# One tile's layernorm statistics moved to ScalarE, a shorter TensorE warm-up and a new matmul order in an FFT-plus-GLU kernel

## Chip, cores and metric

The kernel runs on one core of one Trainium2 chip. The metric is the device time of one execution in microseconds, lower is better. Every run quoted here was fast, with a granted TensorE clock of 0.999 or 1.0 of full speed. A number called "median" is over the executions of one kernel in one comparison; the span of a profile is some 1.8 us shorter than the time of the run that it was taken in.

## The reference, cut to what matters

```python
def reference(A_x, A_w_r, A_w_i, B_x, B_w_gate, B_w_up, B_w_down):
    # A_x: 1 x 2048 x 640 bf16; w_r, w_i: 2048 x 321; w_gate, w_up: 640 x 1536; w_down: 1536 x 640
    xn = _layernorm(A_x, axis=-1)                    # (x - mean) / sqrt(var + 1e-5), per row
    X  = rfft2(xn) * (A_w_r + 1j * A_w_i)            # ... cut: in float32
    a  = irfft2(X)                                   # ... cut
    h  = (xn @ w_gate) * (xn @ w_up)                 # the GLU, F = 1536
    return A_x + a + h @ w_down
```

Everything waits for the layernorm, and TensorE does all the rest: the gated linear unit (GLU), and the Fourier transforms as matmuls with constant tables.

## The kernel before

The source does not list instructions in order. It declares tasks with an engine, an estimated duration, a priority and dependencies, and a list scheduler orders the tasks of each engine and counts PSUM banks for each class of task. The core then runs each engine's list in that order, with semaphore waits (in e8, below, VectorE stood 1.53 us in front of a copy whose input was there). A change to a priority or an estimate therefore changes orders, and nothing else.

Rows 16p+b form tile b, so there are 16 tiles of 128 rows. Tiles 0 to 3 are loaded by one transfer each and transposed by TensorE; tiles 4 to 7 come in one transfer, 8 to 15 in another, and are transposed by DMA. The parts that the change touches:

```python
xv = A_x[0].rearrange("(p j) d -> p j d", j=16)
sch.caps = {"glu": opts.get("cap_glu", 2), "acc": opts.get("cap_acc", 4), "fill": 1}   # PSUM banks per class
# ... cut
for fi in range(opts.get("nfill", 70)):            # filler, planned into early gaps of TensorE
    def em_fill(c):                                # two matmuls of 128 columns on zeros
        # ... cut
nwarm = opts.get("nwarm", 12)
def em_warm(c):                                    # warm-up: 4 * nwarm matmuls of 128 columns on zeros
    # ... cut
T("warm", "pe", opts.get("warm_ns", 5050.0), em_warm, prio=-1.0, ...)
# ... cut: statistics of tile b
if b >= opts.get("act_stats", 6):                  # tiles 6 to 15: two passes on ScalarE
    # activation(Copy, scale=1/640, accum_out=mean), activation(Square, bias=mean, accum_out=sum of squares)
else:                                              # tiles 0 to 5: VectorE, two bn_stats of 320 columns, one bn_aggr
    if 1 <= b <= 3: bns[0].deps.add(muls[b - 1])   # not before the tile ahead is normalised
    if b == 1:      bns[1].deps.add(e0_first)      # second half after tile 0's transposes are copied out
# ... cut: add epsilon (VectorE), square root (ScalarE), reciprocal, subtract, multiply (VectorE)
# T0_b: five transposes of tile b; eT0_b: the copy of them out of PSUM, in two parts for b < 2,
#       columns 0..255 on ScalarE and 256..639 on VectorE
w_at = [6.0 + opts.get("w_rate", 2.2) * min(ft // 2, 4) for ft in range(12)]      # when weights are expected
gu = T("GU_%d_%d" % (ft, b0), "pe", ..., bank="single", cls="glu")                # ten GLU matmuls: 5 gate, 5 up
eg = T("eG_%d_%d" % (ui, u), ("act", "dve"), ..., frees=gu)                       # evacuates them, frees the bank
```

The names used below: a **GLU matmul** is one of GU's matmuls of 128 or 256 columns. The **first length-64 transform** is the first stage of the Fourier part after the early GLU work (L1034 before, L1048 after), some 89 us into the span. From there to the end TensorE does the same matmuls in the same order in both kernels, except for the last few accumulations.

## Time and profile before

| | before |
|---|---|
| time, median of 3 runs | 206.84 us (206.67 to 207.27) |
| span of the profile | 204.3 us |
| TensorE busy | 199.7 us, 98% |
| VectorE, ScalarE busy | 178.7 us, 121.4 us |
| tile 0's transposes start | 6.04 us |
| first GLU matmul | 7.54 us |
| tile 3's transposes start | 14.32 us, after 100 GLU matmuls |
| first length-64 transform | 88.9 us |

The page and the timeline behind this table are shown and read in the prediction. These are rows of the 40 equal slices of the span, 5.1 us each: the busy share of the DMA engines in tenths, and what they moved.

```profile
DMA  6999993603139460001333343225033122324212
GB/s 179 301 342 383 387 210 15 67 0 64 32 66 242 86 202 0 3 0 27 66 65 60 68 113 65 65 70 158 0 98 113 55 76 83 112 80 111 83 35 62
```

From the second to the sixth slice the DMA engines are busy for 90% or more, moving 300 to 390 GB/s for most of it.

### The profile page before, as it was taken

Reading aid. Unit: us, or ns where it says so; the run is one execution under the profiler, and the core shown is the slowest. Engines: PE = TensorE matmul, PEld = TensorE weight load, DVE = VectorE, ACT = ScalarE, POOL = GpSimd, SP = SyncE. Lnnn points to the kernel's source line nnn. Section 1 sums busy time; section 2 is a strip of 40 time slices with the busy share of each in tenths; the row PEclk is TensorE's granted clock in tenths of the full one; section 3 lists DMA queues with packets and bytes.
Section 4 is the critical chain, followed back from the end, with each engine's and each line's share of the span. In section 5 each row is a group of like instructions: output and inputs, shape, how many; then the busy total and the mean of one; then the engine's idle time right before and its main releaser. Section 6 shows DMA issues by size and latency. Waiting matters only on the chain.

```text
span 204.3 us, 4499 instructions
## 1 busy us (share of the span) xinstructions
PE 199.7 (98%) x1681; PEld 137.2 (67%) x1695; DVE 178.7 (87%) x508; ACT 121.4 (59%) x282; POOL 21.8 (11%) x36
## 2 busy tenths in 40 slices
PE   7999999999999999999999999999999999999995
PEld 7998999554545455465777666666777787777774
DVE  3798999999999999949997997818999999999973
ACT  2379998999976577577999899878420222000000
POOL 0000000000000000003655365310000000000000
PEclk9999999999999999999999999999999999999999
DMA  6999993603139460001333343225033122324212
GB/s 179 301 342 383 387 210 15 67 0 64 32 66 242 86 202 0 3 0 27 66 65 60 68 113 65 65 70 158 0 98 113 55 76 83 112 80 111 83 35 62
DMA packets 30740, 21.69 MB, mean 106 GB/s; under 512 B 10752, under 2 KB 29696, under 8 KB 30592
## 3 DMA queue, kind: packets, MB, share of 16 engines
q1 hardware_dynamic: 29920, 21.06, 40.6%
q10 hardware_dynamic: 800, 0.36, 0.6%
q8 instruction: 13, 0.21, 0.4%
q14 instruction: 7, 0.06, 0.1%
HBM read 16.82 MB, written 2.62 MB: 95 GB/s over the span
## 4 chain that ended last, share of the span: by engine, by line
PE 92%; DVE 6%; issue 1%; ACT 1%
PE ps L969 36%; PE ps L1229 26%; PE ps L989 13%; DVE arena L1070 3%; PE ps L747 3%; PE ps L930 2%; PE ps L1146 2%; PE ps L1239 2%; PE ps L1034 2%; PE ps L1117 2%; PE ps L1118 2%; DVE arena L1073 1%; PE ps L1058 1%; PE ps L1055 1%; PE ps L1057 1%; PE ps L1056 1%
## 5 line engine op out<-in xcount | busy, mean ns | idle before, releaser
L719 ACT ACTIVATE arena<-ps 128x512 bf16<-128x512 f32 (+5 forms) x183 | 97.1, 568 | 48.7 <-PE ps L1146 23.4
L969 PE MATMUL ps<-arena 128*128 128x512 bf16 x346 | 80.1, 379 | 0.9 <-DVE arena L1073 0.3
L969 PEld LDWEIGHTS ps<-arena 128*128 128x128 bf16 x360 | 33.9, 98 | 36.5 <-ACT arena L719 0.8
L1229 PE MATMUL ps<-arena 128*128 128x320 bf16 (+2 forms) x396 | 56.7, 295 | 0.0
L1229 PEld LDWEIGHTS ps<-arena 128*128 128x128 bf16 x396 | 38.0, 98 | 13.9
L989 PE MATMUL ps<-arena 128*128 128x128 bf16 (+1 forms) x360 | 28.2, 237 | 0.1
L989 PEld LDWEIGHTS ps<-arena 128*128 128x128 bf16 x360 | 24.9, 98 | 2.5 <-ACT arena L719 0.7
L1070 DVE TENSOR_TENSOR arena<-ps,arena 128x256 f32<-128x256 f32 x64 | 22.6, 414 | 1.4 <-PE ps L1058 1.2
L1005 DVE TENSOR_TENSOR arena<-arena 128x512 bf16<-128x512 bf16 x36 | 15.3, 425 | 9.0 <-ACT arena L719 8.8
L1093 POOL TENSOR_TENSOR arena<-arena 128x256 bf16<-128x256 f32 x16 | 10.3, 644 | 111.5 <-DVE arena L1086 111.5
L1249 DVE TENSOR_TENSOR arena<-ps,arena 128x320 bf16<-128x320 f32 (+2 forms) x33 | 15.3, 473 | 3.8 <-PE ps L1239 3.8
L1094 POOL TENSOR_TENSOR arena<-arena 128x256 bf16<-128x256 f32 x16 | 11.9, 745 | 0.0
L1117 PE MATMUL ps<-arena 128*128 128x128 bf16 x80 | 10.4, 219 | 0.1
L1118 PE MATMUL ps<-arena 128*128 128x128 bf16 x80 | 10.4, 219 | 0.0
L1117 PEld LDWEIGHTS ps<-arena 128*128 128x128 bf16 x80 | 8.7, 111 | 1.7
L1118 PEld LDWEIGHTS ps<-arena 128*128 128x128 bf16 x80 | 8.7, 112 | 1.4
L1239 PE MATMUL ps<-arena 128*128 128x320 bf16 (+2 forms) x33 | 9.1, 295 | 0.0
L883 DVE TENSOR_TENSOR arena<-arena 128x384 f32<-128x384 bf16 x16 | 8.8, 551 | 0.0
L773 ACT ACTIVATE arena<-arena 128x640 bf16<-128x640 bf16 x10 | 8.3, 825 | 0.0
L782 DVE BATCH_NORM_STATS2 arena<-arena 128x6 f32<-128x320 bf16 x12 | 5.4, 481 | 2.8 <-DMA arena<-in_A_x_dram 2.7
L767 ACT ACTIVATE arena<-arena 128x640 bf16<-128x640 bf16 x10 | 7.3, 734 | 0.3 <-DMA arena<-in_A_x_dram 0.2
L1073 DVE TENSOR_TENSOR arena<-ps,arena 128x260 f32<-128x260 f32 x16 | 7.0, 438 | 0.0
(72 smaller groups left out, 235.7 us busy)
## 6 DMA issues: line engine op xcount, KB each, us to landing
arena<-in_A_x_dram SPq DMA_DIRECT2D x20, 160.0 KB, 2.5
out_dram<-arena SPq DMA_DIRECT2D x31, 80.0 KB, 1.6
arena<-c_tf SPq DMA_DIRECT2D x4, 384.0 KB, 11.2
arena<-in_A_w_r_dram SPq DMA_DIRECT2D x32, 40.1 KB, 2.3
arena<-in_A_w_i_dram SPq DMA_DIRECT2D x32, 40.1 KB, 2.3
arena<-in_B_w_gate_dram SPq DMA_DIRECT2D x4, 320.0 KB, 5.4
arena<-in_A_x_dram SPq DMA_DIRECT2D x1, 1280.0 KB, 10.3
arena<-c_ti SPq DMA_DIRECT2D x2, 512.0 KB, 4.9
```

The source lines that it names most:

```text
L719: return c.e.activation(dst, src, _ACTF.Copy)
L969: ins = c.e.matmul(ps[:, bk, :], v_gw[:, w, j, ft, :], v_xt[:, j, rows], start=(j == 0), stop=(j == 4))
L989: ins = c.e.matmul(ps[:, bk, w * n:(w + 1) * n], v_gw[:, w, j, ft, :], v_xt[:, j, rows], start=(j == 0), stop=(j == 4))
L1005: return c.e.tensor_tensor(v_ht[:, ft0, rows], v_gbf[:, rr, 0, :], v_gbf[:, rr, 1, :], _OP.mult)
L1070: c.e.tensor_tensor(v_p[:, ar, w, :, 128 * h:128 * h + 128].rearrange("p c (m k) -> p c m k", k=4), xh.rearrange("p c (m k) -> p c m k", k ...
L1093: c.e.tensor_tensor(v_y[ar][:, 512:768], p01[:, 0:256], p10[:, 0:256], _OP.add)
L1094: return c.e.tensor_tensor(v_y[ar][:, 256:512], p00[:, 0:256], p11[:, 0:256], _OP.subtract)
L1117: c.e.matmul(dst, l1, v_ti[:, t, 0, :], start=True, stop=False)
L1118: ins = c.e.matmul(dst, l2, v_ti[:, t, 1, :], start=False, stop=True)
L1229: ins = c.e.matmul(ps[:, bk, 0:sl3.stop - sl3.start], v_ht[:, ft, a * 128:(a + 1) * 128], v_wd[:, ft, sl3], start=(ft == 7 and px is None) ...
L1239: return c.e.matmul(ps[:, bank_of(own), 0:sl3.stop - sl3.start], v_sm[:, 2, :], v_v[:, a, sl3], start=False, stop=True)
L1249: return c.e.tensor_tensor(v_out[:, a % 2, sl3], ps[:, bk, 0:sl3.stop - sl3.start], v_xr[:, xs, sl3], _OP.add)
```

## The change

Its intent: have TensorE start useful work sooner. Tile 1 is normalised earlier, because its statistics run on ScalarE while VectorE is busy with tile 0; the warm-up ends before tile 0 is ready instead of after it; the filler is cut finer and is tied behind tile 0's transposes; and a third PSUM bank with new priorities lets more 128-column GLU matmuls come early.

```diff
@@ -564,6 +564,7 @@
 
         sch = _Sched()
         sch.caps = {"glu": opts.get("cap_glu", 2), "acc": opts.get("cap_acc", 4), "fill": 1}
+        sch.caps["glu2"] = opts.get("cap_glu2", 3)
         sch.caps["a"] = opts.get("cap_a", 2)
         lay = {}
         cur = [0]
@@ -730,15 +731,18 @@
         def em_wz(c):
             return c.e.memset(v_dum, 0.0)
         T("warm_zero", "dve", 150.0, em_wz, writes=[(b_dum, None)], prio=-1.0)
+        fills = []
         for fi in range(opts.get("nfill", 70)):
             def em_fill(c):
                 bk = bank_of(c.t)
-                c.e.matmul(ps[:, bk, 0:128], v_dum[:, 0:128], v_dum[:, 128:256], start=True, stop=True)
-                return c.e.matmul(ps[:, bk, 128:256], v_dum[:, 0:128], v_dum[:, 128:256], start=True,
-                                  stop=True)
-            T("fill%d" % fi, "pe", 2 * _d_mm(128), em_fill, prio=90.0 + 0.001 * fi, bank="single", cls="fill",
-              selffree=True, reads=[(b_dum, None)])
-        nwarm = opts.get("nwarm", 12)
+                ins = None
+                for i in range(4):
+                    ins = c.e.matmul(ps[:, bk, 64 * i:64 * i + 64], v_dum[:, 0:128], v_dum[:, 128:192], start=True,
+                                     stop=True)
+                return ins
+            fills.append(T("fill%d" % fi, "pe", 2 * _d_mm(128), em_fill, prio=90.0 + 0.001 * fi, bank="single", cls="fill",
+              selffree=True, reads=[(b_dum, None)]))
+        nwarm = opts.get("nwarm", 10)
 
         def em_warm(c):
             bk = bank_of(c.t)
@@ -747,7 +751,7 @@
                 ins = c.e.matmul(ps[:, bk + (i % 2), (i % 4) * 128:(i % 4 + 1) * 128], v_dum[:, 0:128],
                                  v_dum[:, 128:256], start=True, stop=True)
             return ins
-        T("warm", "pe", opts.get("warm_ns", 5050.0), em_warm, reads=[(b_dum, None)], prio=-1.0,
+        T("warm", "pe", opts.get("warm_ns", 4280.0), em_warm, reads=[(b_dum, None)], prio=-1.0,
           bank="pair", cls="warm", selffree=True)
 
         def em_wpad(c):
@@ -759,15 +763,20 @@
             dma("ld_x%d" % gi, v_x[:, b0:b0 + nb, :], xv[:, b0:b0 + nb, :], 128 * nb * (1800 if nb == 4 else 1400 if nb == 1 else 1280),
                 [(b_x, ("s", b0, b0 + nb))], prio=(0.0, 0.003, 0.02, 0.03, 0.042, 0.06)[gi])
         muls = {}
+        sd0 = None
+        aset = set(opts.get("act_set", (1,))) | set(range(opts.get("act_stats", 6), 16))
         for gi, (b0, nb) in enumerate(_LN_GROUPS):
             pbase = 1.0 + 0.05 * gi if gi < 4 else opts.get("ln_prio", 5.99) + 0.05 * (gi - opts.get("ln_lead", 4))
             for b in range(b0, b0 + nb):
-                if b >= opts.get("act_stats", 6):
+                if b in aset:
                     def em_sm(c, b=b):
                         return c.e.activation(v_jk, v_x[:, b, :], _ACTF.Copy, scale=1.0 / _D,
                                               accum_out=v_m32[:, b:b + 1])
-                    T("sm%d" % b, "act", _d_act(640) + 93, em_sm, reads=[(b_x, ("s", b, b + 1))],
+                    sm_ = T("sm%d" % b, "act", _d_act(640) + 93, em_sm, reads=[(b_x, ("s", b, b + 1))],
                       writes=[(b_m32, ("b", b, b + 1)), (b_jk, None)], prio=pbase)
+
+                    if b < 4 and sd0 is not None:
+                        sm_.deps.add(sd0)
 
                     def em_sq(c, b=b):
                         return c.e.activation(v_jk, v_x[:, b, :], _ACTF.Square, scale=-1.0, bias=v_m32[:, b:b + 1],
@@ -784,14 +793,14 @@
                                      writes=[(b_st, ("b", 2 * b + i, 2 * b + i + 1))], prio=pbase))
                     if 1 <= b <= 3:
                         bns[0].deps.add(muls[b - 1])
-                    if b == 1:
+                    if b == 1 and opts.get("bn1_split", 1):
                         bns[1].deps.add(e0_first)
 
                     def em_ag(c, b=b):
                         return c.e.bn_aggr(v_mv[:, b, :], v_st[:, b, :])
                     T("ag%d" % b, "dve", 176.0, em_ag, reads=[(b_st, ("b", 2 * b, 2 * b + 2))],
                       writes=[(b_mv, ("b", b, b + 1))], prio=pbase)
-            if b0 >= opts.get("act_stats", 6):
+            if b0 in aset:
                 def em_mb(c, sl_=slice(b0, b0 + nb)):
                     c.e.tensor_copy(v_mv[:, sl_, 0], v_m32[:, sl_])
                     return c.e.tensor_scalar(v_mv[:, sl_, 1], v_ss[:, sl_], 1.0 / _D, None, _OP.mult)
@@ -806,7 +815,9 @@
 
             def em_sd(c, sl_=sl_):
                 return c.e.activation(v_sd[:, sl_], v_ve[:, sl_], _ACTF.Sqrt)
-            T("sd_%d" % gi, "act", 200.0, em_sd, reads=[(b_ve, gk)], writes=[(b_sd, gk)], prio=pbase - 0.006)
+            sd_ = T("sd_%d" % gi, "act", 200.0, em_sd, reads=[(b_ve, gk)], writes=[(b_sd, gk)], prio=pbase - 0.006)
+            if gi == 0:
+                sd0 = sd_
 
             def em_rs(c, sl_=sl_):
                 return c.e.reciprocal(v_rs[:, sl_], v_sd[:, sl_])
@@ -846,6 +857,9 @@
                     return ins
                 t0 = T("T0_%d" % b, "pe", 5 * _d_mm(128), em_t0, reads=[(b_x, ("s", b, b + 1)), (b_sm, ("t", 0, 1))],
                        prio=pb, bank="pair" if b < opts.get("e0_split", 2) else "single", cls="a")
+                if b == 0:
+                    for f in fills:
+                        f.deps.add(t0)
 
                 if b < opts.get("e0_split", 2):
                     for part, (j0, j1) in (("act", (0, 2)), ("dve", (2, 5))):
@@ -855,7 +869,7 @@
                             src = psb[:, o_: o_ + (j1 - j0) * 128].rearrange("p (j s) -> p j s", s=128)
                             return copy_on(c, v_xt[:, j0:j1, b * 128:(b + 1) * 128], src)
                         n_ = (j1 - j0) * 128
-                        es_ = T("eT0_%d_%s" % (b, part), part, {"dve": _d_dve_psum16(n_), "act": _d_act(n_)}, em_e0s,
+                        es_ = T("eT0_%d_%s" % (b, part), (part, "dve") if part == "act" else part, {"dve": _d_dve_psum16(n_), "act": _d_act(n_)}, em_e0s,
                                 writes=[(b_xta if j0 == 0 else b_xtb, ("s", b * 128, (b + 1) * 128))], prio=pb - 0.001, frees=t0)
                     hold(t0, es_)
                     if b == 0:
@@ -874,7 +888,7 @@
         for g in range(8):
             b = 2 * g
             gr = g % 2
-            pf = opts.get("f_prio", 6.05) + 0.05 * g
+            pf = opts.get("f_prio", 6.0) + 0.05 * g
 
             def em_s1(c, b=b, gr=gr):
                 ins = None
@@ -948,7 +962,7 @@
                     gvs[w_][:, :, f0 * 128:(f0 + nf) * 128], 5 * 128 * nf * (340 if nf == 2 else 280),
                     [(b_gw, ("s", w_ * _NGW + f0, w_ * _NGW + f0 + nf))], prio=(0.004, 0.012, 0.022, 0.032, 0.05)[i] + 0.001 * w_,
                     q="act" if w_ and i < 1 else "sp")
-        w_at = [6.0 + opts.get("w_rate", 2.2) * min(ft // 2, 4) for ft in range(12)]
+        w_at = [6.0 + opts.get("w_rate", 1.8) * min(ft // 2, 4) for ft in range(12)]
         c_at = [6.3 + opts.get("c_rate", 1.8) * (b0 + nb - 1) for b0, nb in _CHUNKS]
         units = sorted((max(c_at[ci], w_at[ft | 1]), ci, ft) for ci in range(len(_CHUNKS))
                        for ft in range(0, 12, 1 if _CHUNKS[ci][1] == 4 else 2))
@@ -992,7 +1006,7 @@
                 gu = T("GU_%d_%d" % (ft, b0), "pe", 10.15 * _d_mm(n), em_gu,
                        reads=[(b_gw, ("s", w_ * _NGW + ft, w_ * _NGW + ft + 1)) for w_ in range(2)] + [
                            (b_xta, ("s", b0 * 128, b0 * 128 + n)), (b_xtb, ("s", b0 * 128, b0 * 128 + n))],
-                       prio=pu + 0.001 * u, bank="single", cls="glu")
+                       prio=pu + 0.001 * u, bank="single", cls="glu2")
 
                 def em_eg(c, gu=gu, rr=rr, n=n, u=u):
                     return copy_on(c, v_gbf[:, rr, u, 0:2 * n], ps[:, bank_of(gu), 0:2 * n])
@@ -1133,7 +1147,7 @@
             dma("ld_wd%d" % f0, v_wd[:, f0:f1], wdv[:, f0:f1], 128 * (f1 - f0) * 1280,
                 [(b_wd, ("e", 640 * f0, 640 * f1))], prio=18.0 if f0 < 7 else 9.6, after=[muls[opts.get("w_after", 15)]])
         for a in range(16):
-            pa = 19.0 + opts.get("i_rate", 0.2) * a
+            pa = 19.0 + opts.get("i_rate", 0.05) * a
             pc = 41.0 + 0.05 * a
             r2 = a % 2
 
@@ -1258,7 +1272,7 @@
         sch.window = 100.0
         sch.urgent = opts.get("urgent", ('T0_0', 'T0_1', 'T0_2', 'T0_3'))
         sch.slack["act"] = opts.get("slack_act", 500.0)
-        sch.slack["dve"] = opts.get("slack_dve", 600.0)
+        sch.slack["dve"] = opts.get("slack_dve", 300.0)
         sch.slack["pe"] = opts.get("slack_pe", 1500.0)
         sch.affinity = opts.get("affinity", 300.0)
         sch.dma_bw = float(opts.get("dma_bw", 380.0))
```

The planned order of TensorE's list at the start changes as follows (counts are matmuls; T0 is a tile's five transposes, GLU ones are of 128 columns where nothing is said):

```
before  warm 48, T0, filler 14, GLU 30, T0, GLU 30, T0, GLU 40, T0, GLU 20, GLU of 256 columns 60, ...
after   warm 40, T0, filler 36 of 64 columns, GLU 20, T0, GLU 50, T0, GLU 40, T0, GLU 50, GLU of 256 columns 80, ...
```

## The prediction

Two of its words: "cold" is the stretch with a load of weights every 105 ns in the mean of the warm-up (5.04 us for 48), and "the clock opens" where they begin to pass every 56 ns, at about 6.8 us in the first profile. The granted clock is 1.00 before and after that point, and what brings the change is not shown. The second spacing is called the full rate below. The 734 and 825 of ScalarE's Copy and Square are ns.

> **What bounds the kernel now.** I read the page first for which engine is full, then the chain of work that ended last for where that engine is not the one that decides, then the timeline of the first 10 us, because every part of the diff that is more than a number acts there.
>
> The busy shares and the chain:
>
> ```profile
> PE 199.7 (98%) x1681; PEld 137.2 (67%) x1695; DVE 178.7 (87%) x508; ACT 121.4 (59%) x282; POOL 21.8 (11%) x36
> ...
> PE 92%; DVE 6%; issue 1%; ACT 1%
> PE ps L969 36%; PE ps L1229 26%; PE ps L989 13%; DVE arena L1070 3%; PE ps L747 3%; PE ps L930 2%; PE ps L1146 2%; PE ps L1239 2%; PE ps L1034 2%; PE ps L1117 2%; PE ps L1118 2%; DVE arena L1073 1%; PE ps L1058 1%; PE ps L1055 1%; PE ps L1057 1%; PE ps L1056 1%
> ```
>
> TensorE is busy for 98% of the span and 92% of the chain. L747 is the warm-up: 3% of the chain that computes nothing. So time is won only by starting useful matmuls earlier or by closing gaps between them.
>
> How much is there to win? From the chain in order of time: 128-column matmuls pass one per 56 ns, 256-column ones one per 109 ns, 512-column ones one per 216 ns (5 in 1.08 us), 320-column ones one per 136 ns (12 in 1.63 us). Multiplied by their counts, the useful matmuls need about 193 us. The span is 204.3. The 11 us between divide into about 7.3 us before the first GLU matmul (7.54 less 0.28 of useful transposes), 2.4 us after the last matmul (201.9 to 204.3), and some 1.7 us of gaps. From 7.54 to 14.81 the engine does 115 matmuls of 128 columns, 6.4 us of work in 7.27 us: **0.85 us of gaps**. From 14.81 to 35.7 I find another 0.55 us the same way, and little after it.
>
> The timeline of the start; columns are start, duration, engine, line and operation, and in brackets the idle time before and what ended it:
>
> ```profile
> 1.05 5.04 PEld L747 LDWEIGHTS ps<-arena 128*128 128x128 bf16 x48 [1.05 <-DVE arena L754]
> ...
> 4.59 0.21 ACT L808 ACTIVATE arena<-arena 128x1 bf16<-128x1 bf16 x1 [1.62 <-DVE arena L804]
> ...
> 5.03 0.39 DVE L826 TENSOR_SCALAR arena<-arena 128x640 bf16<-128x640 bf16 x1
> ...
> 5.53 0.49 DVE L782 BATCH_NORM_STATS2 arena<-arena 128x6 f32<-128x320 bf16 x1
> 6.04 0.58 PEld L844 LDWEIGHTS ps<-arena 128*128 128x128 bf16 x5
> ...
> 6.93 0.38 ACT L719 ACTIVATE arena<-ps 128x256 bf16<-128x256 bf16 x1 [2.12 <-PE ps L844]
> 6.93 0.36 DVE L720 COPY arena<-ps 128x384 bf16<-128x384 bf16 x1 [0.90 <-PE ps L844]
> ...
> 7.32 0.49 DVE L782 BATCH_NORM_STATS2 arena<-arena 128x6 f32<-128x320 bf16 x1
> ...
> 7.54 1.69 PEld L989 LDWEIGHTS ps<-arena 128*128 128x128 bf16 x30
> ...
> 9.03 0.39 DVE L826 TENSOR_SCALAR arena<-arena 128x640 bf16<-128x640 bf16 x1
> ...
> 9.47 0.28 PEld L844 LDWEIGHTS ps<-arena 128*128 128x128 bf16 x5 [0.24 <-DVE arena L826]
> ```
>
> Two things are to be seen. Tile 0 is normalised at 5.42 (5.03 + 0.39), but its transposes (L844) start at 6.04, when the 48 warm-up matmuls end: the warm-up is 0.6 us too long in this run. And tile 1's statistics are cut in two on VectorE, 5.53 and 7.32, with the wait for tile 0's transposes between, so that tile 1 is ready only at 9.42 and TensorE waits 0.24 us for it.
>
> [...] weight loads of the warm-up come every 105 ns (5.04 us / 48), filler ones from about 6.8 us on every 56 ns. The change came 5.7 us after the first matmul here. The page's row of granted clock does not show it: it is full throughout. [...] The trace has a load with every 128-column matmul at 56 ns per pair[...]; no 64-column matmul is in it, so whether they can pass faster than 56 ns is open. [...] The trace has 734 (L767, Copy) and 825 (L773, Square)[...]. One table load is in the trace although Sqrt, Copy and Square all run, so the moved statistics need no second one.
>
> **The change part by part.**
> - *Warm-up 48 to 40 matmuls.* 40 x 105 ns from 1.05 ends at 5.25. The transposes of tile 0 then wait for its normalisation at 5.42 and start at about 5.47 (before, a multiply ending at 9.42 released a transpose at 9.47): 0.57 us earlier.
> - *Evacuating those transposes.* In the order of the changed program both parts go to VectorE, since ScalarE is busy. Before, start of transposes to start of the copies was 0.89 us cold. So 5.47 + 0.89 = 6.36, then about 0.3 and 0.36 us one after the other, minus some overlap: 6.95, against 7.31. The GLU matmuls could start at 7.0.
> - *Filler.* 14 matmuls of 128 columns become 36 of 64, now after the transposes by an explicit dependency (they stood there already). They start at about 6.05 and stand ahead of the GLU in TensorE's order. If columns set their rate: 12 cold ones to 6.7, [...] end 7.4. If the weight load does: 6 cold ones, 30 x 56 ns, end 8.4. **So the GLU starts at about 7.45 or at 8.4**, against 7.54; not at 7.0 in either case.
> - *Tile 1's statistics on ScalarE.* After the square root (4.80): 0.74 + 0.20 for the accumulator read, less overlap, then 0.82 + 0.2: done at about 6.65. On VectorE two small operations (0.3), add epsilon 0.16, subtract 0.38 with the square root beside it, reciprocal 0.16, multiply 0.39: about 8.0. Tile 1 is ready 1.4 us earlier, and VectorE loses two BATCH_NORM_STATS2 and one aggregate (0.98 + 0.2 us) for 0.3. ScalarE was idle from 4.8 to 6.93, so its 1.8 us are free. But only 0.24 us of TensorE's waiting was for tile 1 directly.
> - *Tiles 2 and 3.* They follow on VectorE, some 0.7 us earlier (tile 2's second half still waits for tile 1's copy), which eases later gaps.
> - *Own bank limit of 3 for small GLU units; priorities; the slack of VectorE.* They reorder TensorE's work up to about 87 us: the third pair of gate and up weights is needed after 120 GLU matmuls (about 15 us) instead of 220. Those weights were issued at 7.1 and 7.6 and such loads take about 6 us, so they should be there at 14. From the first length-64 transform (L1034) on, TensorE's order is the same matmul by matmul except for the last few accumulations. The limit of 3 answers waits on evacuation (L989 waited for ScalarE's copies 0.7 us in all).
>
> *Sum.* TensorE's useful work is unchanged. Fast filler: 7.45 + 6.42 + 0.3 of gaps left (my choice, from 0.85) = 14.2 against 14.81, a gain of 0.6; slow filler: 8.4 + 6.42 + 0.2 = 15.0, a loss of 0.2. From 14.8 to 36 I give 0.2 us more of the 0.55. So -0.8 or 0.0, and the middle is -0.4.
>
> **The rivals.** (a) *The filler eats it:* 64-column matmuls with full weight loads run no faster than 128-column ones, and all that is won before 7 us is lost behind 36 of them. For it: a load per matmul; against it: the copied cost formula in the scheduler counts them at half. It makes 206.8 to 207.2. (b) *VectorE takes over:* it is 98% busy from 20 to 60 us, so an earlier TensorE might meet it. Against: the change takes 0.9 us from VectorE, and from 80 to 100 us it has 3 us to spare. It would cut the gain to about 0.2: 206.6. (c) *The clock opens later:* [...] I give it 5%. (d) *The warm-up wasn't in the way in most runs:* [...] 48 warm-up matmuls end before 5.42 anyway and the shortening gains nothing. [...]
>
> **Range and chances.** Middle of the two fillers 206.4; I tilt by 0.1 to the fast one. 206.3 us. One rival against it is +0.9 at most without (c), the best case with all gaps gone -1.2, and the runs of before scatter by 0.6: 205.3 to 207.3. Two per cent is 4.1 us, more than all the idle time of TensorE that the change can reach, so within 2% has 0.97.
>
> **What would show it.** In the changed profile: transposes of tile 0 at about 5.5; [...] first GLU matmul at 7.4 or 8.4; ScalarE's Copy and Square for tile 1 from 4.8 to 6.7; tile 1's multiply ending near 8.0; no wait of tile 1's transposes; TensorE's gaps to 15 us down from 0.85 to about 0.3; the first L1034-type matmul (89.28 before) earlier by the same amount as the end. Wrong would make it: a late clock change, a wait for the third weight pair at 15 us, or new waits for VectorE from 20 to 60 us.

## The result, and the profile after

The changed kernel took **205.72 us** (median of 4 runs, 205.70 to 205.78), the kernel before 207.06 (4 runs, 206.67 to 207.80). The ratio is 0.9932, with a 95% interval of 0.9902 to 0.9961. Ratios here are the mean time of one kernel's fast runs over that of the other's of the same rounds, so not quite the ratio of the medians. It is a gain, but far inside the 2% that count as "same". Measured again later with more runs on one chip (e5 below) the ratio was 0.9965: 205.84 us in the mean against 206.62, a gain of 0.78 us.

The page of the changed kernel, busy shares and chain:

```profile
PE 198.7 (97%) x1695; PEld 136.1 (67%) x1709; DVE 177.6 (87%) x509; ACT 122.8 (60%) x284; POOL 21.8 (11%) x36
...
PE 89%; DVE 5%; DMA 3%; SPq 1%; issue 1%; ACT 0%
PE ps L983 36%; PE ps L1243 26%; PE ps L1003 13%; DMA arena<-in_B_w_up_dram 3%; DVE arena L1084 3%; PE ps L944 2%; PE ps L1160 2%; PE ps L1253 2%; PE ps L1048 2%; PE ps L1131 2%; PE ps L1132 2%; DVE arena L1087 1%; SPq L714 1%; PE ps L1072 1%; PE ps L1069 1%; PE ps L1071 1%
```

The warm-up, 3% of the chain before, is gone from it. In its place stand 3% of a load of up-projection weights and 1% of the queue that issued it. VectorE lost 1.1 us of work and ScalarE gained 1.4.

The timeline of the start after, with the columns that the prediction explains:

```profile
1.05 3.84 PEld L751 LDWEIGHTS ps<-arena 128*128 128x128 bf16 x40 [1.05 <-DVE arena L758]
...
4.59 0.20 ACT L817 ACTIVATE arena<-arena 128x1 bf16<-128x1 bf16 x1 [1.61 <-DVE arena L813]
...
4.89 0.74 ACT L773 ACTIVATE arena<-arena 128x640 bf16<-128x640 bf16 x1
...
5.53 0.29 PEld L855 LDWEIGHTS ps<-arena 128*128 128x128 bf16 x5 [0.63 <-issue]
...
5.75 0.83 ACT L782 ACTIVATE arena<-arena 128x640 bf16<-128x640 bf16 x1
5.78 1.15 PEld L740 LDWEIGHTS ps<-arena 128*128 128x128 bf16 x36
...
6.85 1.13 PEld L1003 LDWEIGHTS ps<-arena 128*128 128x128 bf16 x20
...
7.58 0.39 DVE L837 TENSOR_SCALAR arena<-arena 128x640 bf16<-128x640 bf16 x1
...
8.02 0.28 PEld L855 LDWEIGHTS ps<-arena 128*128 128x128 bf16 x5
...
8.94 3.09 PE L1003 MATMUL ps<-arena 128*128 128x128 bf16 x50 [0.46 <-DMA arena<-in_B_w_up_dram]
...
9.29 0.49 DVE L791 BATCH_NORM_STATS2 arena<-arena 128x6 f32<-128x320 bf16 x1 [1.32 <-DMA arena<-in_A_x_dram]
...
9.70 0.34 DVE L721 COPY arena<-ps 128x384 bf16<-128x384 bf16 x1
...
14.59 0.28 PEld L855 LDWEIGHTS ps<-arena 128*128 128x128 bf16 x5
```

The reader is to see four things. The warm-up ends at 4.9, so tile 0's transposes start as soon as the tile is ready (5.53, not 6.04). Tile 1's Copy and Square run on ScalarE from 4.89 to 6.6, its multiply ends at 7.97 and its transposes follow at 8.02, 1.45 us earlier than before. Then TensorE stops: at 8.94 it has waited 0.46 us for the second pair of up weights, and at 9.29 VectorE has waited 1.32 us for the rows of tile 2. And at 14.59 tile 3's transposes start *later* than before:

```profile
14.32 0.32 PEld L844 LDWEIGHTS ps<-arena 128*128 128x128 bf16 x5
```

This is the same event in the timeline of the kernel before. A lead of 1.45 us at tile 1 has become a lag of 0.27 us at tile 3. What is left of the lead is that 110 GLU matmuls are done by then and not 100. At 56 ns each that is 0.56 us of work, so the changed kernel is about 0.3 us ahead. The first length-64 transform, in the view by line (shortest, median and longest ns, first and last start in us), before:

```profile
L1034 PEld LDWEIGHTS ps<-arena x80: 95/97/98, 88.9 to 127.1; 128*128 128x128 bf16 x80
```

and after:

```profile
L1048 PEld LDWEIGHTS ps<-arena x80: 95/97/98, 88.6 to 126.8; 128*128 128x128 bf16 x80
```

It is 0.3 us earlier, and so is the end of the span (204.0 against 204.3). In this pair of profiles, then, the gain is all made before 15 us. The difference of the timed means is larger than 0.3, so one pair of profiles cannot be the whole account; the experiments add twelve more profiles that reach the same point.

### The profile page after: what moved, and what is told of

Same layout as the page of the kernel before. It is cut to its first block, busy times and chain, and to the rows that moved or that the text cites. A ratio compares the mean times of both kernels' runs of the same rounds, so it can differ in the third digit from the quotient of the medians.

```text
span 204.0 us, 4533 instructions
## 1 busy us (share of the span) xinstructions
PE 198.7 (97%) x1695; PEld 136.1 (67%) x1709; DVE 177.6 (87%) x509; ACT 122.8 (60%) x284; POOL 21.8 (11%) x36
## 4 chain that ended last, share of the span: by engine, by line
PE 89%; DVE 5%; DMA 3%; SPq 1%; issue 1%; ACT 0%
PE ps L983 36%; PE ps L1243 26%; PE ps L1003 13%; DMA arena<-in_B_w_up_dram 3%; DVE arena L1084 3%; PE ps L944 2%; PE ps L1160 2%; PE ps L1253 2%; PE ps L1048 2%; PE ps L1131 2%; PE ps L1132 2%; DVE arena L1087 1%; SPq L714 1%; PE ps L1072 1%; PE ps L1069 1%; PE ps L1071 1%
## 5 line engine op out<-in xcount | busy, mean ns | idle before, releaser
L720 ACT ACTIVATE arena<-ps 128x512 bf16<-128x512 f32 (+4 forms) x181 | 96.7, 572 | 46.0 <-PE ps L1160 23.4
L782 ACT ACTIVATE arena<-arena 128x640 bf16<-128x640 bf16 x11 | 9.1, 826 | 0.0
L773 ACT ACTIVATE arena<-arena 128x640 bf16<-128x640 bf16 x11 | 8.1, 734 | 0.6 <-DMA arena<-in_A_x_dram 0.5
L791 DVE BATCH_NORM_STATS2 arena<-arena 128x6 f32<-128x320 bf16 x10 | 4.5, 481 | 4.0 <-DMA arena<-in_A_x_dram 3.9
```

The lines of the kernel that those rows point to most:

```text
L720: return c.e.activation(dst, src, _ACTF.Copy)
```

## The experiments

**The theory** going in: the gain is made before 15 us, by ScalarE's statistics and the shorter warm-up, and is capped by the loads. **The rivals:** the gain comes from the reordering alone (third bank and priorities); or from the filler or warm-up alone; or it lies after 89 us, in the stage in which both orders are nearly the same. All runs were made on one chip in three calls. The kernel before was run beside them: 206.62 us in the mean over the first two calls, 206.71 over the third.

| label | kernel | mean of 6 runs | ratio to before, 95% interval |
|---|---|---|---|
| e6 | before, once more (control) | 206.83 | 1.0004 (0.9988 to 1.0020) |
| e5 | after, once more | 205.84 | 0.9965 (0.9941 to 0.9989) |
| e1 | after, warm-up of 48 | 206.40 | 0.9991 (0.9968 to 1.0014) |
| e12 | after, old warm-up and old filler | 206.04 | 0.9968 (0.9944 to 0.9992) |
| e4 | after, no filler | 206.20 | 0.9978 (0.9958 to 0.9999) |
| e2 | after, tile 1's statistics on VectorE | 206.92 | 1.0017 (0.9998 to 1.0036) |
| e3 | after, old priorities and 2 banks | 206.81 | 1.0011 (0.9998 to 1.0025) |
| e7 | before, only the statistics moved | 206.73 | 1.0007 (0.9990 to 1.0025) |
| e10 | before, only the third bank | 206.51 | 0.9990 (0.9970 to 1.0009) |
| e9 | after, 2 banks, same orders | 206.11 | 0.9976 (0.9949 to 1.0004) |
| e8 | after, wait for the second weights removed | 206.53 | 0.9998 (0.9981 to 1.0015) |
| e11 | after, five spectral weight slots | 205.82 | 0.9956 (0.9937 to 0.9975) |

One kernel's six runs scatter by 0.1 to 0.6 us (standard deviation), so a difference of less than about 0.5 us between two rows says little by itself.

### e5 and e6: both kernels again

No edit. Expected of after:

> The changed kernel as it is, on the chip of the next three runs. In the first comparison it had 205.70 to 205.78 in four runs, the kernel before 206.67 to 207.80. In the four experiments so far, the kernel before scattered from 206.15 to 207.15 and their profiles differ in when loads land (second pair of weights 8.5 to 9.4 us, a later wait at 16 us, spectral weights at 110 to 130 us). Theory N (landing times differ from run to run): 205.6 to 206.8, scattered like the others, mean 0.5 us under the kernel before. Theory S (the changed kernel is steady, and only the edits of the experiments unsettle it): 205.6 to 205.9 again.

Expected of before:

> The kernel before, submitted as an experiment: a second profile of it, and a control. Ratio to the kernel before 1.000 within its interval; if the interval excludes 1, intervals of the other runs are too narrow by as much. Start of the GLU: 6.6 to 8.1 us, by when the clock opens (first profile: 6.8 us and 7.54 us). If the clock opens early here (before 5.4), the transposes of tile 0 start at 5.5 despite 48 warm-up matmuls.

Measured: 0.9965 and 1.0004. So the gain is real, and it is about 0.8 us, not the 1.3 us of the first comparison. The control's profile is the longest taken of the old order (205.8 us), and it shows how the start can go worse. Its timeline:

```profile
1.05 4.95 PEld L747 LDWEIGHTS ps<-arena 128*128 128x128 bf16 x48 [1.05 <-DVE arena L754]
...
9.10 0.72 PE L989 MATMUL ps<-arena 128*128 128x128 bf16 x10 [0.69 <-DMA arena<-in_B_w_up_dram]
...
9.47 0.89 DVE L782 BATCH_NORM_STATS2 arena<-arena 128x6 f32<-128x320 bf16 x2 [0.50 <-DMA arena<-in_A_x_dram]
...
17.43 0.74 ACT L767 ACTIVATE arena<-arena 128x640 bf16<-128x640 bf16 x1 [0.93 <-DMA arena<-in_A_x_dram]
...
18.80 1.27 PE L989 MATMUL ps<-arena 128*128 128x256 bf16 x10 [0.54 <-ACT arena L719]
```

Here the kernel before meets the wait for the second up weights too (9.10; in its first profile the GLU started late enough, at 7.54, that these weights had landed). The last two lines show something new. ScalarE stands still for 0.93 us until 17.43, because the next operation in its list is the Copy for the statistics of tile 6, whose rows have not landed; the evacuations of GLU banks stand behind it in the list; and TensorE then waits 0.54 us for a bank, until 18.80, released by ScalarE.

### e1 and e12: is it the warm-up or the filler?

```diff
# e1, from after
-        nwarm = opts.get("nwarm", 10)
+        nwarm = opts.get("nwarm", 12)
-        T("warm", "pe", opts.get("warm_ns", 4280.0), ...
+        T("warm", "pe", opts.get("warm_ns", 5050.0), ...
# e12: the same, and the filler of before, two matmuls of 128 columns without the dependency on T0_0
```

> The changed kernel with its old warm-up of 48 matmuls back; all else as changed. In the profile of the changed kernel the second pair of gate and up weights lands at 8.9 us, and TensorE has waited 0.6 us for it. Theory P (pinned: what happens before those weights land is free, the gain is that tile 1 is ready when they land): 8 more warm-up matmuls cost 0.45 to 0.85 us before 6.1 us, the wait at 8.3 us shrinks by as much, and the time stays within 0.2 us of the changed kernel (205.7). Theory W (the gain is the shorter warm-up): 0.4 to 0.6 us longer, 206.2.

> The changed kernel with both the old warm-up (48) and the old filler (14 of 128 columns, no dependency): what is left is ScalarE statistics, bank limit and order. If the warm-up and the filler are worth nothing: ratio as the changed kernel's in the last call, 0.995 to 0.998. If they are worth 0.3 us or more: 0.998 to 1.000.

Measured: e1 206.40, e12 206.04 us. By itself e1 looks as if the shorter warm-up were worth 0.56 us (206.40 less 205.84), though the interval of that difference includes zero. But e12 has the same long warm-up and the old filler as well, and it keeps the gain: 0.9968 against 0.9965 for the whole change. So **the gain does not need the shorter warm-up and the finer filler**. That they add nothing at all is not shown: e12 and e5 differ by 0.2 us in the mean, and the 95% interval of that difference is some 0.6 us to either side. The start and the later part of e12's timeline:

```profile
5.49 0.29 PEld L853 LDWEIGHTS ps<-arena 128*128 128x128 bf16 x5 [0.17 <-issue]
...
14.24 0.28 PEld L853 LDWEIGHTS ps<-arena 128*128 128x128 bf16 x5
...
14.48 5.04 PEld L1001 LDWEIGHTS ps<-arena 128*128 128x128 bf16 x70
...
16.83 0.74 ACT L771 ACTIVATE arena<-arena 128x640 bf16<-128x640 bf16 x1 [0.49 <-DMA arena<-in_A_x_dram]
```

With 48 warm-up matmuls tile 0's transposes start at 5.49, because the array reached its full rate early in this execution (loads of weights come every 107 ns up to 4.44 us and every 56 ns from there). In e1's profile, whose 48 warm-up loads took 4.03 us against 5.04 in the kernel before, the change came at 3.9, an estimate from that time and the two spacings. So neither profile shows what the long warm-up costs in the new order when the change comes late. From 14.48 on, 70 GLU loads of weights pass without a gap, although ScalarE waits for tile 6 here as well (16.83).

### e4: no filler

```diff
-        for fi in range(opts.get("nfill", 70)):
+        for fi in range(opts.get("nfill", 0)):
```

> The changed kernel with no filler matmuls at all (36 of 64 columns taken out). Theory P: TensorE starts the GLU some 0.2 us earlier and then waits that much longer for the weights that land at 8.9, time within 0.1 us of the changed kernel (205.7)[...]. Theory F (filler delays the useful work): 0.2 us faster, 205.5.

Measured: 206.20 us, ratio 0.9978. Without filler no second slow stretch is seen (from 9.38 us on 50 GLU loads of weights pass in 2.90 us, against 2.94 for 50 in the changed kernel, from 8.91), and nothing was won: in its profile the first GLU matmul waited for its own gate weights until 7.10, and so came no earlier than in the other late starts. In this profile the place of the filler is empty, so the filler takes time from nothing there, and 64-column matmuls pass quickly in any case (in the changed kernel's profile 36 from 5.78 to 6.85, 30 ns each).

### e2: the new priorities without the moved statistics

```diff
-        aset = set(opts.get("act_set", (1,))) | ...
+        aset = set(opts.get("act_set", ())) | ...
```

> The changed kernel with tile 1's statistics back on VectorE (the two BATCH_NORM_STATS2 around tile 0's copy); warm-up, filler, bank limit and priorities as changed. Theory P: tile 1's transposes are then what TensorE waits for after 30 GLU matmuls, they depend again on when tile 0's transposes ran, so on when the clock opened: most of the gain goes, 206.4 to 207.1 us, and the rounds scatter by 0.5 us or more. Theory W: little is lost, 205.7 to 206.0. Theory K (bank limit and order make the gain): little is lost too.

Measured: 206.92 us, the slowest row: 1.08 us more than e5, with an interval of some 0.65 us to either side. Read alone, it says that the new priorities are worth nothing without ScalarE's statistics. Two things warn against reading it alone. With other statistics the scheduler made another order: up to tile 3's transposes the trace has GLU 30, 30 and 40, as before the change, and behind them 60 of 128 columns. And in its timeline:

```profile
16.95 0.74 ACT L773 ACTIVATE arena<-arena 128x640 bf16<-128x640 bf16 x1 [0.44 <-DMA arena<-in_A_x_dram]
...
17.09 4.16 PE L1003 MATMUL ps<-arena 128*128 128x128 bf16 x49 [0.89 <-issue]
```

At 17.09 TensorE stands idle for 0.89 us in the middle of a group of matmuls. The program has no wait there, and the trace names none ("issue"). The cause is not shown. Up to that point this kernel was no later than the changed one (tile 3 at 13.93 with 100 GLU matmuls done, which makes 14.49 at 110). Had all six runs this stall, the mean without it would be 206.03, that of the changed kernel; only one of them has a profile. So e2 does not cleanly show what the statistics are worth in the new order, and **that part stays open**.

### e3 and e7: the moved statistics without the new order

```diff
# e3, from after
-pf = opts.get("f_prio", 6.0) ...        +pf = opts.get("f_prio", 6.05) ...
-w_rate 1.8, i_rate 0.05, slack_dve 300  +w_rate 2.2, i_rate 0.2, slack_dve 600
-    ... bank="single", cls="glu2")      +    ... bank="single", cls="glu")
# e7, from after: the same, and warm-up and filler of before; leaves only the statistics of tile 1 on
# ScalarE and both parts of the copy free to go to VectorE
```

> The changed kernel with the old shared bank limit, priorities, weight and spectral rates and VectorE slack; warm-up, filler and ScalarE statistics as changed. Theory P: at most 0.2 us longer than the changed kernel, 205.7 to 205.9. Theory K: the gain is the order and the third bank, so it goes: 206.6 to 207.0.

> The kernel before with one part of the change: tile 1's statistics on ScalarE (both parts of tile 0's copy then on VectorE); warm-up 48, old filler, old priorities and bank limit. Theory P (tile 1 ready early is the gain): 0.3 to 0.6 us faster than the kernel before, ratio 0.997 to 0.9985. Theory K (order and the third bank make it, since e3 without them lost to the kernel before): ratio 1.000 to 1.002.

Measured: 1.0011 and 1.0007. **The statistics alone gain nothing**, with the new warm-up or with the old. The timeline of e7 shows where the lead goes:

```profile
14.62 0.28 PEld L853 LDWEIGHTS ps<-arena 128*128 128x128 bf16 x5
...
15.88 4.33 PE L1001 MATMUL ps<-arena 128*128 128x256 bf16 x36 [0.24 <-ACT arena L720]
...
16.72 0.74 ACT L771 ACTIVATE arena<-arena 128x640 bf16<-128x640 bf16 x1 [0.62 <-DMA arena<-in_A_x_dram]
```

At 14.62 it stands where the changed kernel stands: tile 3's transposes, 110 GLU matmuls done. But the old priorities put only 10 more of 128 columns behind them, and then groups of 256 columns, which work on tiles 2 and 3. The first of these waits until 15.88. The trace names line L720 of ScalarE, and that is a helper's line: it evacuates GLU banks, and it also copies transposed tiles out of PSUM. ScalarE's timeline in a narrow window, 15.2 to 15.6, tells which it was:

```profile
15.12 0.70 ACT L720 ACTIVATE arena<-ps 128x640 bf16<-128x640 bf16 x1
```

640 columns of bf16 are the copy of tile 3's transposes. It ends at 15.82, just before TensorE goes on; the last evacuation of a bank before it had ended at 15.13. So TensorE waits for tile 3 itself, not for a bank, and its weight loads stand still for 0.41 us. Waits for a bank come later: ScalarE waits 0.62 us for tile 6 at 16.72 with evacuations behind, and at 19.38 the loads stand still for another 0.30 us. In e3 it is the same: 0.41 us for tile 3's copy at 15.82, then 0.28 and 0.31 us until ScalarE frees a bank. The new order has 50 matmuls of 128 columns, 2.8 us of work on tiles 0 and 1, between tile 3's transposes and the first group that needs tile 3. What it changes is not the work but how much of it can be done before tile 3's copy is needed. Counted from the starts of the matmuls, the gaps from 14.8 to 20 us add up to 0.6 us in e7 and 0.8 in e3, and to 0.0 to 0.3 in after, e5, e9, e11 and e12. That these gaps are all that the old order loses is argued, not tested.

### e9 and e10: the third PSUM bank

```diff
# e9, from after
-sch.caps["glu2"] = opts.get("cap_glu2", 3)
+sch.caps["glu2"] = opts.get("cap_glu2", 2)
# e10, from before: adds sch.caps["glu2"] = 3 and uses that class for the GLU matmuls of 128 and 256 columns
```

> The changed kernel with a limit of 2 instead of 3 banks for the small GLU groups; TensorE's and ScalarE's orders are the same instruction by instruction, only waits differ. In the profiles, ScalarE stands still from about 16.5 to 17 us for x of tiles 4 to 7 (its Copy for tile 6 is next in its order) and frees no banks; old-order kernels lose 0.6 to 0.7 us of TensorE there in three of four profiles, the changed kernel 0.0 and 0.2. If the third bank bridges that: this one loses it too, 206.3 to 206.8, with a gap at 15 to 20 us. If the order alone does it: as the changed kernel, ratio 0.995 to 0.998.

> The kernel before with one part of the change: three banks for the small GLU groups. If the third bank is the cause: ratio to before 0.996 to 0.998, and the gap at 15 to 20 us at most 0.2. If the order (wider groups moved later) is needed: ratio 0.999 to 1.001 and the gap stays.

Measured: 0.9976 and 0.9990; both intervals include 1. With two banks the scheduler makes the same order on every engine (the traces of e9 and of the changed kernel agree instruction by instruction), and the time cannot be told from that of the changed kernel. The limit of two did not hold TensorE up behind tile 3: in e9's profile 70 GLU loads pass from 14.49 on in 5.05 us without a wait, as 70 in 4.93 us do in the changed kernel's. With the third bank alone, e10, no gap is seen behind tile 3, but the kernel also starts late:

```profile
14.75 0.32 PEld L845 LDWEIGHTS ps<-arena 128*128 128x128 bf16 x5
...
15.03 4.98 PEld L990 LDWEIGHTS ps<-arena 128*128 128x128 bf16 x56
```

Here 56 loads pass without a wait after 15.03, but tile 3 comes at 14.75 with only 100 GLU matmuls done. ScalarE did not wait for tile 6 in this profile, so it does not test whether the third bank would bridge such a wait. The time is that of before within the noise.

### e8: take the wait for the second weights away

The GLU groups of tile 0 for the third and fourth block of F read the weights of the first and second. The result is wrong on purpose (the run is recorded as correct all the same, so the check does not notice it); the orders of all engines stay the same.

```diff
+                fw = ft - 2 if (b0 == 0 and ft in (2, 3)) else ft
+
-                def em_gu(c, ft=ft, n=n, rows=rows):
+                def em_gu(c, ft=fw, n=n, rows=rows):
```

> The changed kernel, wrong on purpose: the third and fourth GLU groups of rows of the first tile use the first pair of weights, so TensorE doesn't wait for the second pair at 8.3 us (0.6 us in the profile). If that wait costs what it lasts: 0.5 to 0.6 us faster than the changed kernel in this call. If the next load takes its place (x of tile 2 landed at 9.29 us there, tile 2 is normalised at 11.9, and its transposes already wait 0.2 us): that wait grows from 0.2 to about 0.8 us and the time changes by less than 0.2 us.

Measured: 206.53 us, 0.7 us *more* than e5, where the theory that this wait costs 0.6 us wanted less. The timeline says why it gained nothing:

```profile
9.51 0.49 DVE L791 BATCH_NORM_STATS2 arena<-arena 128x6 f32<-128x320 bf16 x1 [1.53 <-DMA arena<-in_A_x_dram]
9.92 0.34 DVE L721 COPY arena<-ps 128x384 bf16<-128x384 bf16 x1
...
10.40 1.83 PE L1005 MATMUL ps<-arena 128*128 128x128 bf16 x30 [0.80 <-DVE arena L721]
```

The wait for weights was gone, and TensorE ran on into a wait for tile 1's copy, 0.80 us. The transposes behind that copy were done by 8.5 us. The copy ran at 9.92 all the same, because VectorE's list has tile 2's BATCH_NORM_STATS2 ahead of it, and that waited 1.53 us for the rows of tile 2. So VectorE kept to the order of its list, with 1.53 us of standing still in front of a copy whose input was there. The same order is in the changed kernel, whose copy ran at 9.70, hidden behind the wait for the weights. So **two loads, the second up weights and tile 2, end within half a microsecond of each other (8.94 and 9.29 us in the changed kernel), and taking one away leaves the other**. Why the run ended later than e5 rather than level is seen in part: VectorE waited another 1.41 us for the rows of tile 3, until 13.56, and tile 3 was transposed only at 16.05. Why those rows came later than in the changed kernel is open.

### e11: five slots for spectral weights

```diff
-_NW = 4
+_NW = 5
```

> The changed kernel with five slots instead of four for the spectral weights, so that each of their loads may be issued one step earlier; TensorE's order is the same. Profiles so far differ by 0.7 us between the first length-64 transform and the end although the order there is the same in all; where they lose, TensorE waits for in_A_w_i loads at 110 to 130 us. If those landings make the scatter: that wait goes, 0.2 to 0.5 us faster on average than the changed kernel and less scatter. If the loads come late for another reason (they stand behind other loads in the queue): no difference.

Measured: 205.82 us, level with e5 (205.84). This tests the rival that the gain or its scatter lies after 89 us. In some profiles TensorE waits there for a transfer of spectral weights, as the view of waits of e1 from 100 to 135 us shows (us of waiting, times, longest):

```profile
PEld ps L1069 <- DMA arena<-in_A_w_i_dram: 0.7, 1, 0.7
```

With five slots no such wait is in the profile. The mean did not move. Its six runs lie closer together (standard deviation 0.13 against 0.55 us), but the four runs of the changed kernel in the first comparison lay within 0.08 us, so that the fifth slot steadies the time is not shown.

### All profiles together

For each profile but e8's (its edit let TensorE run ahead of the weights) I took the start of tile 3's transposes, brought to the same work by adding 0.56 us where only 100 GLU matmuls were done by then, and the time from there to the first length-64 transform. Both are in us.

| group | profiles | tile 3, at 110 GLU matmuls | from there to the first length-64 transform | first length-64 transform |
|---|---|---|---|---|
| old statistics, old order | before, e6, e10 | 14.88, 15.04, 15.31 | 74.0, 74.8, 73.8 | mean 89.3 |
| ScalarE statistics, old order | e7, e3 | 14.62, 14.57 | 74.5, 74.7 | mean 89.2 |
| ScalarE statistics, new order | after, e5, e9, e11, e12, e1, e4 | 14.59, 14.31, 14.25, 14.40, 14.24, 15.24, 14.99 | 74.0, 74.1, 74.1, 74.1, 74.1, 73.7, 73.7 | mean 88.6 |
| old statistics, new priorities | e2 | 14.49 | 75.1, with the 0.89 us stall | 89.6 |

Up to tile 3 the groups with ScalarE's statistics are half a microsecond ahead of the first (means 15.1 and 14.6). But that is not shown to be the statistics' doing: in the three profiles of the first group the array reached its full rate late, at 5.8 to 6.8 us, with the long warm-up, so tile 0's transposes began at about 6.0 and not at 5.5; e2, with the old statistics, the short warm-up and an early change (3.7 us), is at 14.49. In the old order the next stage takes 74.2 and 74.6 us in the mean, in the new order 74.0, and there the lead reaches the first length-64 transform: 0.7 us. These are means of three, two and seven profiles, and within the first group alone the stage varies by 0.9 us. From there to the end of the span the first three groups take the same in the mean, 115.6 to 115.7 us (115.3 to 116.1 one by one). In e1 and e4, where the second weights landed latest (9.12 and 9.38 us), tile 3 is late and the next stage is shorter by the same amount; e8, with tile 3 at 16.05, takes 73.7 us too. I read this as waits for later loads that then no longer occur, which is argued and not tested.

The clearest evidence is in the timed runs. The six kernels that have both the new order and ScalarE's statistics (e5, e1, e12, e4, e9, e11) take 206.07 us in the mean of 36 runs; the two with the statistics in the old order (e3, e7) take 206.77 in 12; the kernel before 206.66 in the 22 that ran beside them.

## Why the prediction was right, point by point

The predicted time was 206.3 us and the measured 205.72, inside the range, and "within 2%" was right. The gain was predicted as 0.54 us (206.84 less 206.3); measured were 1.34 at first and 0.78 in the longer comparison. Several steps on the way were wrong.

- **Tile 0's start: right.** Predicted 5.47, measured 5.53. But the gain does not need it: e12 has the old warm-up and is 0.9968 of the kernel before, against 0.9965 for the whole change. The prediction's rival (d), that the warm-up isn't in the way in most runs, named this; what the profiles add is that in two of the three where the long warm-up did end late (e6, e10) TensorE's weight loads still stood 0.8 us for the second up weights, until 9.1 and 9.3, so an earlier start would have met the same wait.
- **ScalarE's part: right.** Copy and Square were to run from 4.8 to 6.65 and took 0.74 and 0.83 us from 4.89; tile 1's multiply was to end at 8.0 and ended at 7.97.
- **The filler: the fast branch held.** The prediction left open whether 64-column matmuls pass faster than the 56 ns of a 128-column one; the 36 took 1.07 us from 5.78 to the first GLU load at 6.85, 30 ns each, so they do. Its 7.4 for the fast branch rested on a rate that no trace had shown by then. That the first GLU matmul came at 6.85 and not at 7.45 is due to when the full rate came: the prediction took over the late change of the first profile (about 6.8 us), and in this profile it came at about 4.5. In e5, where it came at about 6.4, the GLU started at 7.24.
- **The gaps up to 15 us: the step that failed.** The prediction chose to cut them from 0.85 to 0.3 us, although only 0.24 us of waiting was for tile 1 directly, and named the *third* pair of weights at 15 us as what might go wrong. The third pair was in time. In this profile the *second* pair was not, nor was tile 2: TensorE waited 0.46 us and VectorE 1.32 us. By the prediction's own measure (from the first GLU load to the end of tile 3's transposes, less 56 ns for each matmul) the gaps of the changed kernel are 1.2 us and not 0.3, and those of e5 0.5. The lead shows up as ten more GLU matmuls by tile 3, not as earlier events. That the sum for this point, 14.2, came near the measured 14.5 (15.04 less ten matmuls) is partly luck: the GLU started 0.6 us earlier than predicted, and the gaps were 0.9 us larger.
- **"They reorder TensorE's work": undervalued.** The prediction gave the new order and the third bank 0.2 us of gaps from 14.8 to 36 us and otherwise no term. The runs show that the gain needs it: with the statistics in the old order nothing is left (e7, 1.0007; e3, 1.0011). That it is enough by itself is not shown (e2). The third bank is not the part of it that matters (e9, e10).
- **The end moves with the first length-64 transform: right** in the first pair (0.3 and 0.3 us). What was not foreseen is that the stage after it varies by 0.7 us between profiles, in part by waits for spectral weights such as the 0.7 us in e1.
- **The rivals:** the filler did not eat the gain, VectorE did not take over (from 20 to 60 us TensorE is busy for 39.8 of 40 us before and after), and no profile here showed a second stretch of slow loads at the start, not even without filler (e4: 50 loads in 2.90 us).

What stays open: what the statistics are worth in the new order (e2's stall), how much the warm-up is worth when the full rate comes late, whether the third bank is worth a few tenths of a microsecond, and why e8 ended later than e5.

## What to carry to other kernels

When an engine gets ready sooner at the start of a kernel, look in the trace at which loads land just behind the wait you remove: here the lead lasted only until the next of them (0.46 us of waiting at 8.94), and it was kept only where the order behind it gave the engine work that needs neither a late load nor a copy still being made. Look at the shape of what released a wait before calling it a wait for a buffer: a helper's line can stand for several tasks. An operation that waited for a load held up everything behind it in its engine's list (0.93 us on ScalarE in e6, 1.53 us on VectorE in e8), so it may pay to put evacuations of PSUM ahead of statistics whose rows may be late; no run here tried that. And when a change has several parts, run each part alone and each part taken away: here neither the statistics alone nor the third bank alone showed a gain, the showy part (the warm-up) was not needed for it, and together they made 0.3 to 0.7%.

## What the traces show of the hardware

- By the spacing of weight loads the change from 107 to 56 ns came at about 6.8 and 5.8 us in two profiles of the kernel before, at about 4.5 and 6.4 us in two of the changed one, and at 3.7 us in e2, with the first matmul at 1.05 each time: 2.7 to 5.7 us after it. The granted clock in the profiles of before and after is 1.00 throughout. After the change, pairs of a weight load and a 128-column matmul passed every 56 ns, and pairs with 64 columns every 30 ns (36 from 5.78 to 6.85 us), so a load per matmul did not hold these to 56 ns.
- On ScalarE an ACTIVATE with an accumulator output is followed by an instruction of its own, ACTIVATION_READ_ACCUMULATOR, which takes 0.18 to 0.21 us in these traces.
- The landing of the same load varies between executions. TensorE's wait for the second up weights, issued at 2.7 us in before and in e2, ended at 8.54 us in e2, at 9.10 in e6 and at 9.41 in e4, and the rows of tiles 4 to 7 let ScalarE go on at 16.52 us in before and at 17.43 in e6. That spread is as large as the effect that was studied.
